# Block-sparse attention and a channel mixer in one kernel: PSUM as four slots of two banks for everything

## The chip, the cores and the metric

The kernel runs on one core of a Trainium2 chip, as one launch. The metric is the device time of that launch in microseconds (us). The engines are named as in the profile: PE (TensorE, the matmuls), ACT (ScalarE), DVE (VectorE), POOL (GpSimd) and SP (SyncE, which issues most DMAs). PSUM, where PE writes its results, has eight banks of 512 fp32 columns on 128 partitions.

## The reference

For 4 batches, 8 heads, 768 tokens and a head size of 64, attention with a block mask (blocks of 32 tokens), then a mixer over tokens and channels:

```python
scores = scale * np.matmul(q, k.transpose(0, 1, 3, 2))
mask = ...            # neighbours, first and last block, three sampled blocks per row of blocks
attn = softmax(np.where(mask, scores, -1e9))
x = np.matmul(attn, v) # heads side by side: batch, 768 tokens, 512 channels

h = x.transpose(0, 2, 1) @ U @ V          # rank 32, over the tokens
u = x + h.transpose(0, 2, 1)
out = u + np.maximum(u @ w_ch1, 0.0) @ w_ch2   # 512 -> 2048 -> 512 channels
```

## The kernel before, in words

Two heads are a pair; there are 16 pairs, four to a batch. Tokens are taken as six tiles of 128. All matmuls are in fp16 and add up in fp32.

- **Q K^T.** A pair is nine steps (`score`, L397): steps 0 to 5 take one key tile against queries 0 to 511, steps 6 to 8 take two key tiles against queries 512 to 767. Both heads of a step use 64 rows of the array each and write one PSUM tile of two banks. ACT takes exp of the whole step (L412, 128 x 1024) into an `e` buffer. In batch 0 the mask is added on PE (L404); later DVE multiplies `e` by the mask (L440, L445).
- **E V.** `values` (L478) multiplies a step's `e` with v, eight matmuls of 65 columns, the last column being the sum of the softmax. The pair's result lies in two accumulator tiles, one for token tiles 0 to 2 and one for 3 to 5. `divide` (L505, L508) divides on DVE into `x32`, and a copy to fp16 (`x16`, L524) follows. For the last pair of batch 0 DVE writes `x16` first and then `x32`, both from PSUM.
- **Token mix.** `amix` (L542) makes `a16` from x16 and U for a group of pairs (the first three pairs of a batch, then the fourth). `umix` transposes one block of 128 channels of x16 (L558) and adds V times a16 (L562), in two halves of 384 tokens; each half has its own PSUM tile and is copied to `uT` (L568) by ACT or DVE.
- **Channel products.** `up` (L592) multiplies w_ch1 with uT: for each two of the 16 rows of 128 channels three parts of 512 columns, each with a PSUM bank of its own and a Relu by DVE (L604) or ACT (L606) into `tT`. `down` (L615, L618) takes one token tile at a time through w_ch2, and DVE adds x32 (L625). The very last token tile goes in two halves (`down_half`, L637, L639).

PSUM is two tiles of two banks for the scores and four single banks for all else. The order is written out by a planner in the source: it keeps an estimated clock for each engine and for the banks (`take`, `give`, `drop`), and at each point issues the piece with the best rank that could start by then: a Q K^T visit, an E V visit, a mix piece or a channel piece. The instructions then run on each engine in that order; semaphores hold an instruction until what it needs is there. Once channel products are under way a Q K^T visit is two steps, held back by a due time so that the visits spread over the products. An E V visit is then six steps, or three. Batch b's products run among batch b+1's attention; the last batch's run alone at the end.

Of the kernel before, what the change touches and what calls it, by code (L numbers as in the profile page):

```python
# [22 lines left out]
def kernel(  # L23
# [32 lines left out]
    EB = 14  # L56
# [33 lines left out]
    tpool = ctx.enter_context(tc.tile_pool(name="tpool", bufs=9))  # L90
# [4 lines left out]
    ps_s = ctx.enter_context(tc.tile_pool(name="ps_s", bufs=2, space=PS))  # L95
    ps_f = ctx.enter_context(tc.tile_pool(name="ps_f", bufs=4, space=PS))

    def bank(shape, dtype):
        return ps_f.tile(shape, dtype, tag="ff", name="ff")
# [100 lines left out]
    def build_allow():  # L200

        pm = bank([P, NT, NB], FP32)
        for t in range(NT):
            nc.tensor.matmul(
                pm[:, t], biasf[:, t : S : NT], id16[:, 0:NB], start=True, stop=True
            )
        nc.vector.tensor_scalar(out=allow_k, in0=pm, scalar1=-1.0, scalar2=None, op0=ALU.is_ge)
# [31 lines left out]
    def keep_busy(n, cols):  # L239

        if not idle:
            idle.append(bank([P, 512], FP32))
        for _ in range(n):
            nc.tensor.matmul(
                idle[0][:, 0:cols], warm[:, 0:P], warm[:, 0:cols], start=True, stop=True
            )
# [37 lines left out]
    def transpose_part(name, t0, t1, evict):  # L284

        st = staged[name, 0]
        if t0 == 0:
            first[name] = new_qkT(name, 0)
        pt = bank([P, t1 - t0, P], FP16)
        for t in range(t0, t1):  # L290
            nc.tensor.transpose(  # L291
                out=pt[:, t - t0, :], in_=st[:, t].rearrange("p h d -> p (h d)"), identity=id16
            )
        evict(out=first[name][:, t0:t1], in_=pt)
# [41 lines left out]
    banks = [0.0, 0.0, 0.0, HELD]  # L336

    def take(n=1):
        banks.sort()
        return banks[n - 1]  # L340

    def give(t):

        banks.sort()
        banks[0] = t

    def drop(t):

        banks.sort()
        assert banks[-1] == HELD  # L350
        banks[-1] = t
# [7 lines left out]
    t_e, t_qk, t_x = {}, {}, {}  # L359
    sc_free = [0.0, 0.0]  # L360
# [28 lines left out]
    def score(si):  # L389
        n, s = divmod(si, SPP)  # L390
        qT, kT = qkT["q", n], qkT["k", n]
        sc_free.sort()
        ps = ps_s.tile([P, 2, 512], FP32, tag="sc", name="sc")
        biased = 2 <= si < SPB
        for g, q0, nq, at in parts(n, s):
            for h in range(2):
                nc.tensor.matmul(  # L397
                    ps[:, h, at : at + nq],
                    kT[h * D : (h + 1) * D, g * P : (g + 1) * P],
                    qT[h * D : (h + 1) * D, q0 : q0 + nq],  # L400
                    start=True, stop=not biased,
                )
            for h in range(2 if biased else 0):
                nc.tensor.matmul(  # L404
                    ps[:, h, at : at + nq],
                    biasf[h * D : (h + 1) * D, g : S : NT],
                    qhot[h * D : (h + 1) * D, q0 : q0 + nq],
                    start=False, stop=True,
                )
        t = on_pe(1024 if biased else 512, "rows", t_qk[n], sc_free[0], t_bias[0] if biased else 0.0)  # L410
        e = epool.tile([P, 2, 512], FP16, tag="e", name="e")
        nc.scalar.activation(out=e, in_=ps, func=AF.Exp, scale=0.125)  # L412
        sc_free[0] = t = on("ACT", 1024, t)
        if biased:
            t_e[si] = t
        else:
            masks.append((t, si, e))
            t_e[si] = max(t, clk["DVE"]) + FIX["DVE"] + COL["DVE"] * 1024 * 0.55 + HOP
        etiles[si] = e
# [32 lines left out]
    def values(sis):  # L452
# [9 lines left out]
        if n not in accs:  # L462
            if idle:
                idle.clear()
                drop(0.0)
            need = max(need, take(2))
            give(HELD)
            give(HELD)
            accs[n] = [0, [bank([P, NT // 2, 2, D + 1], FP32) for _ in range(2)], [0, 0]]
# [19 lines left out]
        if acc[0] == SPP:  # L489
            divide(n, 1, acc[1][1], t)  # L490
            del accs[n]

    def divide(n, hf, acc, t):
# [22 lines left out]
        if n == NPR - 1:  # L516

            t_x[n] = times(x16)
            drop(times(x32))
        else:  # L520
            t = times(x32)
            drop(t)
            eng = pick(nt * P, t, engines=("POOL", "DVE" if n < NPR else "ACT"))
            COPY[eng](out=x16[:, ts, c], in_=x32[:, ts, c])  # L524
            t_x[n] = on(eng, nt * P, t)

# [3 lines left out]
    def mixing(b, p0, p1):  # L530
# [8 lines left out]
        def amix():  # L539
            pa = bank([P, np_ * P], FP32)  # L540
# [10 lines left out]
        def umix(c, hf):  # L551

            if hf == 0:
                uT[c] = utp.tile([P, S], FP16, tag="uT", name="uT")
            pu = bank([P, HS], FP32)
            cs = slice(c * P, (c + 1) * P)
            for i in range(NT // 2):
                nc.tensor.matmul(  # L558
                    pu[:, i * P : (i + 1) * P], x16[:, hf * (NT // 2) + i, cs], id16,
                    start=(i == 0), stop=False,  # L560
                )
            nc.tensor.matmul(  # L562
                pu, a16[:, cs], Vt.rearrange("r t p -> r (t p)")[:, hf * HS : (hf + 1) * HS],
                start=False, stop=True,
            )
            tt = on_pe(HS * 2.3, "full", tm["a16"], take())
            eng = pick(HS, tt)
            COPY[eng](out=uT[c][:, hf * HS : (hf + 1) * HS], in_=pu)  # L568
            tm["uT"] = on(eng, HS, tt)
# [4 lines left out]
            (lambda: max(take(), tm["a16"]), lambda c=c, hf=hf: umix(c, hf))  # L574
            for c in range(p0, p1) for hf in range(2)
# [4 lines left out]
    def channels(b, uT, x32, a16, tm):  # L580
# [3 lines left out]
        def up(j, part):  # L584

            if part == 0:
                tT.append(tpool.tile([P, 2, S], FP16, tag="tT", name="tT"))
            pt = bank([P, 512], FP32)
            todo = [(part, 0, QA, 0)] if part < 2 else [(0, QA, QB, 0), (1, QA, QB, QB)]
            for i, q0, nq, at in todo:  # L590
                for c in range(NC):
                    nc.tensor.matmul(  # L592
                        pt[:, at : at + nq],
                        w1t[:, c, (2 * j + i) * P : (2 * j + i + 1) * P], uT[c][:, q0 : q0 + nq],
                        start=(c == 0), stop=(c == NC - 1),
                    )
            tt = on_pe(NC * 512, "full", tm["uT"], take())
            if part < 2:
                dst, src_ = tT[j][:, part, 0:QA], pt
            else:  # L600
                dst, src_ = tT[j][:, :, QA:S], pt.rearrange("k (i q) -> k i q", i=2)
            eng = pick(512, tt)
            if eng == "DVE":
                nc.vector.tensor_scalar_max(out=dst, in0=src_, scalar1=0.0)  # L604
            else:
                nc.scalar.activation(out=dst, in_=src_, func=AF.Relu)  # L606
            t_t[0] = on(eng, 512, tt)
            give(t_t[0])

        def down(t, j4):  # L610
            if j4 == 0:
                hold["at"] = take()
                give(HELD)
                hold[t] = bank([P, HD], FP32)
                nc.tensor.matmul(hold[t], Vt[:, t, :], a16, start=True, stop=False)  # L615
                on_pe(HD, "full", hold["at"])
            for j in range(JD * j4, JD * j4 + JD):
                nc.tensor.matmul(  # L618
                    hold[t], tT[j // 2][:, j % 2, t * P : (t + 1) * P], w2t[:, j, :],
# [3 lines left out]
            if j4 == NJ // JD - 1:  # L623
                of = opool.tile([P, HD], FP32, tag="of", name="of")
                nc.vector.tensor_add(out=of, in0=x32[:, t], in1=hold.pop(t))  # L625
                nc.sync.dma_start(
                    out=out[b].rearrange("(p t) c -> p t c", t=NT)[:, t, :], in_=of
                )
                drop(on("DVE", HD, tt))

        def down_half(t, hf):
# [4 lines left out]
            ph = bank([P, HD // 2], FP32)  # L636
            nc.tensor.matmul(ph, Vt[:, t, :], a16[:, c], start=True, stop=False)  # L637
            for j in range(NJ):
                nc.tensor.matmul(  # L639
                    ph, tT[j // 2][:, j % 2, t * P : (t + 1) * P], w2t[:, j, c],  # L640
# [10 lines left out]

        pieces = [
            (lambda: max(tm["uT"], take()), lambda j=j, part=part: up(j, part))
            for j in range(NJ // 2) for part in range(3)
        ]
        pieces += [
            ((lambda: max(t_t[0], take())) if j4 == 0 else (lambda: 0.0),
             lambda t=t, j4=j4: down(t, j4))
            for t in range(NT) for j4 in range(NJ // JD)
        ]  # L660
        if b == B - 1:
            pieces[-(NJ // JD) :] = [
                (lambda: max(t_t[0], take()), lambda hf=hf: down_half(NT - 1, hf))
# [38 lines left out]
    UP, DOWN = NC * 512, JD * HD  # L702
    NUP, NDOWN = 3 * NJ // 2, NT * NJ // JD
    FFN = NUP * UP + NDOWN * DOWN
    SPARE = 28000

    def left():

        d = min(len(chan), NDOWN)
        return d * DOWN + (len(chan) - d) * UP  # L710

# [3 lines left out]
    while step < NSTEP or ai < NSTEP or mixes or chan or waiting or groups:  # L715
# [13 lines left out]
        if step < NSTEP:  # L729
            n = step // SPP  # L730
            if n in t_qk and step - freed_steps() < EB:
                free = min(sc_free)
                if chan:

                    due = (step - SPB * (chan_done + 1)) / SPB * (FFN - SPARE)
                    free = max(*sc_free, now + due - (FFN - left()))

# [5 lines left out]
        if ai < NSTEP:  # L743
            n, at = divmod(ai, SPP)
            r = n % NPR
            end = n * SPP + (NW if at < NW else SPP)
# [6 lines left out]
            if todo and (ai + len(todo) == end or full or not chan):  # L753
                if not chan:
# [8 lines left out]
                if ok:  # L763
                    cands.append((rank, max(when, 0.0 if n in accs else take(2)), "av"))
# [6 lines left out]
        if what == "qk":  # L771
# [16 lines left out]
            for _ in range(2 if chan else 1):  # L788
# [51 lines left out]
```

## Time and profile before

| | |
|---|---|
| time, median of 3 runs | 299.05 us (298.02 to 299.06) |
| the profiled execution | 298.72 us, its span 296.8 us |
| granted PE clock | 0.999 |
| Q K^T matmuls, L397 | 384, busy 48.2 us; mask bias L404 92, 14.4 us |
| E V matmuls, L478 | 1152, busy 44.7 us |
| channel products, L592 and L618 | 512 and 368, busy 88.7 and 88.6 us |
| exp, L412 | 144, busy 138.7 us, 1025 ns each |
| Relu, L604 on DVE and L606 on ACT | 48 each, 690 and 597 ns each |

Matmuls are pipelined: the profile's duration of one (380 ns for 512 columns) is longer than the distance from one start to the next (216 ns), so busy shares of PE overstate, and the starts in the timeline tell what a stretch costs. In a group's row the last number is the engine's idle time just before those instructions, followed by what ended most of it; in the timeline a bracket gives the same for one entry. "Waits" lists give engine, tile and line that waited, what for, the sum in us, the number of waits and the longest.

### The profile page before, as it was taken

The numbers are of one execution on the slowest core, as the hardware profiler recorded it, in microseconds if no ns is written. First come the engines' busy times: TensorE is split into PE (matmuls) and PEld (weight loads), VectorE is DVE, ScalarE is ACT, GpSimd is POOL, SyncE is SP. The second block draws the span as 40 slices with busy tenths as digits, with TensorE's granted clock in tenths as the row PEclk, the third lists the DMA queues.
The fourth block names the chain that finished last, engine by engine and source line by source line (L and its number), as shares of the span: only waits on it lengthen the run. The fifth ranks groups of instructions, "written<-read, shape, count | busy, mean of one in ns | idle before, by whom it ended". The sixth has DMA issues, their size and how long they took to land.

```text
span 296.8 us, 6527 instructions
## 1 busy us (share of the span) xinstructions
PE 288.6 (97%) x2774; PEld 158.3 (53%) x2774; DVE 171.6 (58%) x308; ACT 183.2 (62%) x233; POOL 59.8 (20%) x75
## 2 busy tenths in 40 slices
PE   7998998999999999999999999999999999999995
PEld 2454654565635555565635555565645555665444
DVE  5662246787885666678775766678855664000112
ACT  4898977767655755767665664777666562664000
POOL 3734745230270403012040304003010000000000
PEclk9999999999999999999999999999999999999999
DMA  6689999999977428070356528061201101000111
GB/s 184 205 191 217 235 236 196 275 151 142 201 222 150 135 71 253 0 210 6 62 189 101 184 65 256 1 153 61 55 35 38 38 36 73 0 0 2 71 71 71
DMA packets 46596, 35.90 MB, mean 121 GB/s; under 512 B 26400, under 2 KB 43600, under 8 KB 46568
## 3 DMA queue, kind: packets, MB, share of 16 engines
q1 hardware_dynamic: 41056, 30.94, 41.4%
q0 software_dynamic: 5152, 4.39, 9.9%
q8 instruction: 21, 0.34, 0.5%
q10 hardware_dynamic: 360, 0.17, 0.2%
q14 instruction: 7, 0.06, 0.1%
HBM read 27.59 MB, written 6.29 MB: 114 GB/s over the span
## 4 chain that ended last, share of the span: by engine, by line
PE 90%; DMA 4%; ACT 3%; issue 1%; POOL 0%; DVE 0%; ACTq 0%; POOLq 0%
PE ff L592 29%; PE ff L618 27%; PE sc L397 12%; PE ff L478 11%; ACT e L412 3%; DMA raw_k<-in_k_dram 2%; PE ff L558 2%; PE ff L615 2%; PE ff L542 2%; PE ff L562 2%; PE sc L404 1%; DMA kT<-st_k 1%; PE ff L639 1%; DMA raw_q<-in_q_dram 1%; PE ff L291 0%
## 5 line engine op out<-in xcount | busy, mean ns | idle before, releaser
L412 ACT ACTIVATE e<-sc 128x1024 f16<-128x1024 f32 x144 | 138.7, 1025 | 23.8 <-PE sc L397 19.5
L592 PE MATMUL ff<-uT,w1t 128*128 128x256 f16 (+1 forms) x512 | 88.7, 326 | 0.4 <-ACT uT L568 0.4
L618 PE MATMUL ff<-w2t,tT 128*128 128x512 f16 x368 | 88.6, 379 | 0.0
L592 PEld LDWEIGHTS <-w1t 128*128 128x128 f16 x512 | 47.9, 98 | 38.8 <-issue 8.6
L440 DVE TENSOR_TENSOR e<-e,mask 128x1024 f16<-128x1024 f16 x74 | 55.4, 777 | 3.0 <-ACT e L412 2.9
L618 PEld LDWEIGHTS <-tT 128*128 128x128 f16 x368 | 34.1, 98 | 41.2 <-issue 5.5
L397 PE MATMUL sc<-qT,kT 64*128 64x512 f16 (+1 forms) x384 | 48.2, 327 | 1.9 <-DMA kT<-st_k 1.5
L478 PEld LDWEIGHTS <-e 128*128 128x128 f16 x1152 | 39.6, 97 | 16.1 <-issue 9.5
L478 PE MATMUL ff<-v,e 128*128 128x65 f16 x1152 | 44.7, 193 | 0.3 <-ACT e L412 0.3
L625 DVE TENSOR_TENSOR of<-x,ff 128x512 f32<-128x512 f32 x23 | 15.8, 687 | 48.6 <-PE ff L618 48.6
L604 DVE TENSOR_SCALAR tT<-ff 128x512 f16<-128x512 f32 x48 | 32.8, 690 | 15.7 <-PE ff L592 15.2
L606 ACT ACTIVATE tT<-ff 128x512 f16<-128x512 f32 x48 | 28.7, 597 | 21.4 <-PE ff L592 21.1
L146 POOL CAST st_q<-raw_q 128x768 f16<-128x768 f32 x15 | 13.8, 921 | 104.1 <-DMA raw_q<-in_q_dram 79.4
L524 ACT CAST x<-x 128x384 f16<-128x384 f32 x21 | 10.7, 512 | 35.0 <-DVE x L508 35.0
L397 PEld LDWEIGHTS <-kT 64*128 64x128 f16 x384 | 14.7, 94 | 20.5 <-issue 13.9
L445 DVE TENSOR_TENSOR e<-e,mask 128x1024 f16<-128x1024 f16 x36 | 24.3, 688 | 1.7 <-ACT e L412 1.7
L505 DVE RECIPROCAL rcp<-ff 128x6 f32<-128x6 f32 x32 | 6.2, 195 | 29.3 <-PE ff L478 28.9
L508 DVE TENSOR_TENSOR x<-ff,rcp 128x384 f32<-128x384 f32 (+1 forms) x34 | 18.8, 557 | 1.2
L137 POOL CAST v<-raw_v 128x768 f16<-128x768 f32 x16 | 15.0, 937 | 11.6 <-DMA raw_v<-in_v_dram 9.3
L146 POOL CAST st_k<-raw_k 128x768 f16<-128x768 f32 x15 | 13.3, 888 | 8.2 <-DMA raw_k<-in_k_dram 7.9
L404 PE MATMUL sc<-qhot,bias 64*128 64x256 f16 (+1 forms) x92 | 14.4, 320 | 0.0
L568 DVE CAST uT<-ff 128x384 f16<-128x384 f32 x18 | 9.7, 554 | 5.6 <-PE ff L562 5.4
(60 smaller groups left out, 121.6 us busy)
## 6 DMA issues: line engine op xcount, KB each, us to landing
raw_v<-in_v_dram SPq DMA_DIRECT2D x16, 384.0 KB, 5.9
out_dram<-of SPq DMA_DIRECT2D x23, 256.0 KB, 2.0
raw_q<-in_q_dram SPq DMA_DIRECT2D x15, 384.0 KB, 3.7
raw_k<-in_k_dram SPq DMA_DIRECT2D x15, 384.0 KB, 4.6
w1t<-in_moe_w_ch_dram POOLq DMA_DIRECT2D x4, 512.0 KB, 10.6
w2t<-in_moe_w_ch_dram POOLq DMA_DIRECT2D x4, 512.0 KB, 15.4
raw_q<-in_q_dram SPq DMA_DIRECT2D x1, 256.0 KB, 3.4
raw_k<-in_k_dram SPq DMA_DIRECT2D x1, 256.0 KB, 4.9
```

Source lines behind the costliest of these rows:

```text
L146: nc.gpsimd.tensor_copy(out=st, in_=raw[name, n].rearrange("p h (t d) -> p t h d", d=D))
L397: nc.tensor.matmul(ps[:, h, at : at + nq], kT[h * D : (h + 1) * D, g * P : (g + 1) * P], qT[h * D : (h + 1) * D, q0 : q0 + nq], start=True ...
L404: nc.tensor.matmul(ps[:, h, at : at + nq], biasf[h * D : (h + 1) * D, g : S : NT], qhot[h * D : (h + 1) * D, q0 : q0 + nq], start=False, s ...
L412: nc.scalar.activation(out=e, in_=ps, func=AF.Exp, scale=0.125)
L440: nc.vector.tensor_mul(out=e, in0=e, in1=m)
L445: nc.vector.tensor_mul(out=ev, in0=ev, in1=m)
L478: nc.tensor.matmul(acc[1][hf][:, t % (NT // 2), h, :], e[:, h, at + t * P - q0 : at + t * P - q0 + P], vt[:, g, h, 0 : D + 1], start=(done ...
L508: nc.vector.tensor_tensor(out=x[:, ts, c].rearrange("q t (h d) -> q t h d", d=D), in0=acc[:, :, :, 0:D], in1=rcp[:, :, :, None].broadcast_ ...
L592: nc.tensor.matmul(pt[:, at : at + nq], w1t[:, c, (2 * j + i) * P : (2 * j + i + 1) * P], uT[c][:, q0 : q0 + nq], start=(c == 0), stop=(c ...
L604: nc.vector.tensor_scalar_max(out=dst, in0=src_, scalar1=0.0)
L606: nc.scalar.activation(out=dst, in_=src_, func=AF.Relu)
L618: nc.tensor.matmul(hold[t], tT[j // 2][:, j % 2, t * P : (t + 1) * P], w2t[:, j, :], start=False, stop=(j == NJ - 1),)
```

## The change

PSUM becomes one pool of four slots, each of two banks, for scores, accumulators, mixes and products alike. A Q K^T visit among products is three steps, and goes as soon as the planner's estimate has slots for them and for the next product; the due time is gone. E V among products takes all nine steps of a pair in one visit, into the two banks of one slot. `umix` puts 512 tokens in bank 0 and 256 in bank 1 of one slot, each copied out as soon as it is written. `up` takes four rows of channels at a time in three parts, each part in a slot of its own (two halves of eight matmuls, one Relu of 1024 columns for both), and `down` takes two token tiles to a slot, with one add and one output DMA for both. The `e` buffers go from 14 to 16. The core of the diff (names and planner only lines left out):

```diff
-    EB = 14
+    EB = 16
...
-    ps_s = ctx.enter_context(tc.tile_pool(name="ps_s", bufs=2, space=PS))
-    ps_f = ctx.enter_context(tc.tile_pool(name="ps_f", bufs=4, space=PS))
-
-    def bank(shape, dtype):
-        return ps_f.tile(shape, dtype, tag="ff", name="ff")
+    ps = ctx.enter_context(tc.tile_pool(name="ps", bufs=4, space=PS))
+
+    def slot(dtype=FP32):
+
+        return ps.tile([P, 2, 512 if dtype == FP32 else 1024], dtype, tag="ps", name="ps")
...
-            accs[n] = [0, [bank([P, NT // 2, 2, D + 1], FP32) for _ in range(2)], [0, 0]]
+            both = slot()[:, :, 0 : NT * (D + 1)].rearrange("q i (t h d) -> q i t h d", h=2, d=D + 1)
+            accs[n] = [0, [both[:, i] for i in range(2)], [0, 0]]
...
-        def umix(c, hf):
-
-            if hf == 0:
-                uT[c] = utp.tile([P, S], FP16, tag="uT", name="uT")
-            pu = bank([P, HS], FP32)
+        def umix(c):
+
+            uT[c] = utp.tile([P, S], FP16, tag="uT", name="uT")
+            both = slot()
             cs = slice(c * P, (c + 1) * P)
-            for i in range(NT // 2):
+            ends = []
+            for q0, q1, eng in ((0, QA, "ACT"), (QA, S, "DVE")):
+                pu = both[:, q0 // QA, 0 : q1 - q0]
+                for t in range(q0 // P, q1 // P):
+                    nc.tensor.matmul(
+                        pu[:, t * P - q0 : (t + 1) * P - q0], x16[:, t, cs], id16,
+                        start=(t * P == q0), stop=False,
+                    )
                 nc.tensor.matmul(
-                    pu[:, i * P : (i + 1) * P], x16[:, hf * (NT // 2) + i, cs], id16,
-                    start=(i == 0), stop=False,
+                    pu, a16[:, cs], Vt.rearrange("r t p -> r (t p)")[:, q0:q1],
+                    start=False, stop=True,
                 )
...
+                if b > 0 or c < NPR - 1:
+                    eng = pick(q1 - q0, tt)
+                COPY[eng](out=uT[c][:, q0:q1], in_=pu)
...
-        def up(j, part):
+        def up(j, part, half):
...
+            if half == 0:
+                hold["at"] = take()
+                give(HELD)
+                hold["up"] = slot()
+            pt = hold["up"]
+            if part < 2:
+                todo = [(2 * part + half, 0, QA, 0)]
+            else:
+                todo = [(2 * half + i, QA, QB, i * QB) for i in range(2)]
...
-            eng = pick(512, tt)
+            eng = pick(1024, tt)
...
-        def down(t, j4):
+        def down(t, i, n, j4):
...
+                of = opool.tile([P, 2, HD], FP32, tag="of", name="of")
+                nc.vector.tensor_add(out=of[:, 0:n], in0=x32[:, ts], in1=po[:, 0:n])
                 nc.sync.dma_start(
-                    out=out[b].rearrange("(p t) c -> p t c", t=NT)[:, t, :], in_=of
+                    out=out[b].rearrange("(p t) c -> p t c", t=NT)[:, ts, :], in_=of[:, 0:n]
                 )
...
                 if chan:
 
-                    due = (step - SPB * (chan_done + 1)) / SPB * (FFN - SPARE)
-                    free = max(*sc_free, now + due - (FFN - left()))
+
+                    free = max(take(i + 1) - 512 * i for i in range(size + chan[0][2]))
...
-            end = n * SPP + (NW if at < NW else SPP)
+            end = (n + 1) * SPP
...
-            for _ in range(2 if chan else 1):
+            for i in range(size):
```

In the changed kernel the lines are: Q K^T L395 (bias L402), exp L410, masks L439 and L444, E V L477, `divide` L504 and L507, `amix` L541 (copy L546), `umix` L559 and L563 (copies L570), `up` L601 (Relu L616 and L618), `down` L630 and L633 (add L641), `down_half` L653.

## The prediction

> **What bounds the kernel now.** I read the page first: busy shares, then the chain that ended last.
>
> ```profile
> PE 288.6 (97%) x2774; PEld 158.3 (53%) x2774; DVE 171.6 (58%) x308; ACT 183.2 (62%) x233; POOL 59.8 (20%) x75
> PE 90%; DMA 4%; ACT 3%; issue 1%; POOL 0%; DVE 0%; ACTq 0%; POOLq 0%
> ```
>
> TensorE (PE) is the chain. No other engine is above 62%, so anything taken from or given to ACT and DVE alone is worth nothing; what counts is PE time and PE waiting. The waits of PE say how much waiting there is to win:
>
> ```profile
> PE sc L397 <- DMA kT<-st_k: 1.5, 1, 1.5
> PE ff L592 <- ACT uT L568: 0.4, 1, 0.4
> ```
>
> These are the first and third of that list; behind 49 us there is practically nothing. So a gain must come from PE work itself, and a new PE wait has nothing that hides it. Next, the PE timeline from 49 us on:
>
> ```profile
> 49.41 2.11 PE L592 MATMUL ff<-uT,w1t 128*128 128x512 f16 x13 [0.40 <-ACT uT L568]
> 51.46 0.61 PE L397 MATMUL sc<-qT,kT 64*128 64x512 f16 x4
> 52.00 2.77 PE L592 MATMUL ff<-uT,w1t 128*128 128x512 f16 x16
> 54.70 0.61 PE L397 MATMUL sc<-qT,kT 64*128 64x512 f16 x6
> ```
>
> A visit of Q K^T (L397, 64-row tiles) lasts 51.46 to 52.00, 0.54 us, for two steps whose matmuls stream in 2 x 0.216 = 0.43. The sixteen L592 behind it need 8 x 0.216 + 8 x 0.109 = 2.60 (starts of single matmuls) and take 2.70. By single starts, going into L397 costs 96 ns and coming out 92: 0.19 us a visit. That is the one PE cost this change reduces.
>
> **What it removes.** The instruction order of both kernels, cut at the first L592, shows 53 Q K^T visits behind it before and 36 after: 17 x 0.188 = **-3.2 us**. Two more unmasked steps (39 before, 41 after) stand ahead of that cut: 2 x 0.22 = **-0.44** behind it. All other matmuls, in columns and number, stay. E V in one visit saves nothing on PE: L478 to L592 shows no switching cost (L478's own 29 ns spacing goes on).
>
> **Off the path, taken at nothing.** Relu evictions halve in number and double in size (ACT 48 x 0.597 becomes 24 x 1.03; DVE 48 x 0.69 becomes 24 x about 1.22, an estimate from 0.690 for 512 and 1.04 ns a column). L592 hides them: a slot is filled in 1.73 us. If that cover went, each costs at most 0.5 more than now. The output adds and SP's output DMAs fall to about half; loads and transposes on SP keep their order. The last token still goes in two halves, so the tail behind PE (3.6 us) stays.
>
> **What it adds: a PE wait inside every channel mix.** Here the order with its semaphore waits decides. In `umix` both banks of one slot are filled, but the copy out of bank 0 is emitted before the transposes into bank 1. In the changed kernel's PE queue all 16 umix look like this:
>
> ```
> 2098 L563 Matmult ps_1727<-Vt_128,a16_1668 128x512
> 2100 L559 Matmult ps_1727<-id16_99,x16_1258 128x128 [waits DVE_49]
> ```
>
> The engine waited for is each time the one that copies bank 0 (ACT nine times, DVE seven), and the value awaited is the count which that copy itself reaches: dependence is kept by tile, and the slot is one tile. Before, the halves were two tiles:
>
> ```profile
> 44.47 0.33 PE L562 MATMUL ff<-Vt,a 128*128 128x384 f16 x1
> 44.63 0.33 PE L558 MATMUL ff<-id,x 128*128 128x128 f16 x3
> 44.83 1.22 DVE L568 CAST uT<-ff 128x384 f16<-128x384 f32 x2 [0.67 <-PE ff L562]
> 48.86 0.50 ACT L568 CAST uT<-ff 128x384 f16<-128x384 f32 x1
> 49.41 1.79 PE L592 MATMUL ff<-uT,w1t 128*128 128x512 f16 x10 [0.40 <-ACT uT L568]
> ```
>
> PE is at the next half (44.63) before DVE starts on the first (44.83), 0.36 us behind a 384-column start. And PE resumes 0.05 us behind a copy (48.86 + 0.50, 49.41). So the new wait is: 0.42 (0.36 plus 128 more columns) + the copy + 0.05, less the 0.216 that the matmul streams anyway. The copy of 512 columns:
>
> ```profile
> L604 DVE TENSOR_SCALAR tT<-ff 128x512 f16<-128x512 f32 x48 | 32.8, 690 | 15.7 <-PE ff L592 15.2
> L606 ACT ACTIVATE tT<-ff 128x512 f16<-128x512 f32 x48 | 28.7, 597 | 21.4 <-PE ff L592 21.1
> ```
>
> So 0.94 us for DVE and 0.84 for ACT, if that engine is free. PE executes in order: Q K^T, E V and the products queue behind it, and no work covers it.
>
> Batches 1 to 3, first three umix together (order: three steps, L633 x4, L541 x6, L633 x4, umix). With 0 at the three steps' start, ACT ends its third exp at 0.42 + 3 x 1.025 = 3.5 and is wanted at 4.1; DVE's masks end at 4.9 and it is wanted at 5.6. No queueing: ACT, DVE, ACT = 0.84 + 0.94 + 0.84 = 2.62, times 3 = 7.9.
> The fourth umix of each batch: batch 1, ACT is on the third exp until 3.5, wanted at 3.4, so 0.91, less 0.17 that L592 waited for uT before (spacing 385 instead of 216). Batch 2: the product queue is empty here (two one-step visits around L541 instead of products), so PE also waits about 0.1 for x16 and 0.48 for a16 behind an exp, then 0.94, less 0.17: 1.35. Batch 3: from L541's start to the first full-speed L592, 0.85 + 0.42 + 0.59 + 0.05 + 0.22 = 2.13 after against 1.52 before: 0.61. Together 2.7. Sum **+10.6**.
>
> **Batch 0, from its first L541 to L592.** Before this is 37.28 to 48.77 (L592's first three, then 0.56 waiting). The order after has L541 one step earlier, about 36.4. From there PE has, by rows, L541 1.4, nine Q K^T visits 5.4, eight E V steps 1.95, umix 2.64: 11.4 us of work. Its waits: three umix on DVE 2.8; the last one on ACT, behind an exp, 1.2; and a second wait of the same kind in E V, whose bank 1 steps wait until L507 has read bank 0 twice (reciprocal 0.20, 2 x 0.56, 0.2 to start): 1.5; x16 and a16 0.6. So 17.5, L592 at 53.9 against 48.77: **+5.1**. ACT, which sets the pace until 36 us (eleven exps in 10.19 us), has by then only one exp in reserve, so I take little of it as hidden; the same E V wait of pairs 0 to 2 (about 0.4 each) lies under the exps and costs nothing.
>
> **Do four slots suffice?** No row shows it. Walking the products behind the first L592 by rows, slots come free just in time: a third step starts at 5.61 and its slot is free at 5.43; E V wants one at 15.39, free at 15.2. Bounds: 0, and half an exp (0.5) at each of 36 visits, 18 us. The walk is nearest to 0, and a PE held up by umix only gives the slots more time: 0, with 3 us in the range.
>
> **The sum.** Profiled execution 298.72 (span 296.8 plus 1.9; the median is 299.05): 298.72 - 3.2 - 0.44 + 10.6 + 5.1 = **310.8 us**.
>
> **Rivals.**
> 1. *The bank-1 waits cost nothing* (faster). Then 298.7 - 3.2 - 0.4 = 295.1. For it: before, PE wrote one bank while DVE read another. The Trainium skill, page "PSUM — Partial Sum Buffer", section "PSUM bank collisions raise a hardware error", says guarding by bank and 32-partition quadrant is enough, and that different banks do not collide; a guard by its rule would give this rival's time, 295. The overlap at 44.8 agrees. Against it: the wait is in the built queue and names the copy. It decides if a wait is under 3.6 / 16 = 0.23 us; 0.42 of latency alone is more. Chance 0.07 (0.05 faster, 0.02 near zero).
> 2. *Slots run dry as well.* A third step half an exp late at every visit gives 310.8 + 18 = 329, at a third of them 317. It decides if copies come 0.2 later than my walk. The evenly spread exps speak for it, 36 visits without pacing against. Chance 0.10.
> 3. *Batch 0's waits hide under the exps.* ACT idles several times 0.5 us from 36 to 48 us, which speaks against. Then 310.8 - 5.1 = 305.7. Chance 0.06.
> 4. *PE's clock drops behind the pauses.* The first L244 matmuls stand 427 ns apart, later ones 216; eight such at 16 places would add 1.7 each, 338. Against it: granted clock 1.00 in every stretch, and full speed right behind a 1.66 us pause at 23.85. On the pages, "TensorE: Matmul & The Clock Gate", section "A second HAM failure mode: psum-queue depth-cycling", in the Trainium skill, speaks for this: short pauses between groups that cycle through banks were seen to throttle the clock. The 1.66 us pause here does not agree. Chance 0.02.
>
> The forecast has 0.75.
>
> **Range.** Low: batch 0's term halved (-2.6) and waits shorter by 0.2 each (-2.7): 305.5. High: slots 3 and 0.2 queueing on each of 12 umix, 2.4: 316.5. It leaves out rivals 1 and 4 and most of 2. A measurement of this kernel tells about 0.5% (1.5 us) from no change. Faster 0.05, same 0.02, slower 0.93.
>
> **What would show it.** In the profile after: PE waits with a new line L559 <- ACT and DVE L570, some 14 us in 16 pieces of 0.8 to 1.4; L477 <- DVE L507 about 1.5 at 45 us; first L601 near 54 us; L395 in 36 visits behind it, 0.19 saved each. Wrong if L559 waits under 4 us in sum, or if L395 or L601 wait for ACT L410 for several us.

## The result: 312.44 us, 4.5% slower

The changed kernel takes 312.44 us (median of six executions, 311.14 to 313.82), the kernel before 299.06 beside it (298.02 to 303.49): 1.045 times the time, interval 1.0405 to 1.050. The ratios here and below leave out executions more than 1.5% above the fastest of their kernel. The profiled execution took 313.55 us, its span 311.6. From the page of the kernel after, busy time and the chain that ended last:

```profile
PE 287.6 (92%) x2774; PEld 160.0 (51%) x2774; DVE 157.1 (50%) x261; ACT 192.4 (62%) x224; POOL 55.4 (18%) x72
...
PE 83%; ACT 4%; DVE 3%; DMA 1%; issue 1%; ACTq 0%
```

PE has the same 2774 matmuls and is even busy 1.0 us less than before, yet its share of the chain fell from 90% to 83%: the 15 us came mostly as waiting. The waits of PE in the kernel after (engine, tile, line, what for; sum in us, number, longest) say where:

```profile
PE ps L559 <- ACT uT L570: 6.5, 9, 1.1
PE ps L559 <- DVE uT L570: 5.5, 7, 0.8
PE ps L477 <- DVE x L507: 2.3, 4, 1.3
PE ps L395 <- DMA kT<-st_k: 1.9, 1, 1.9
...
PE ps L395 <- ACT e L410: 0.8, 2, 0.5
PE ps L559 <- ACT e L410: 0.4, 1, 0.4
```

The first two lines are new: 9 + 7 = 16 waits, one in each `umix`, each for the copy of bank 0 of the slot whose bank 1 is to be written. One of them, in the chain of the kernel after (start, duration):

```profile
104.90 0.23 PE ps L563
105.13 0.02 issue
105.16 0.59 ACT uT L570
105.75 0.04 issue
105.79 0.27 PE ps L559 x2
```

PE starts the matmul that ends bank 0 at its own rate (104.74 by the timeline; the chain shows it where the one before ends), the copy starts 0.42 us behind that start, lasts 0.59, and PE goes on 0.04 us behind it at 105.79. Without the wait the next transposes would have started 0.22 behind 104.74, at 104.96: 0.83 us lost. The list of waits counts less than that, because it takes a matmul as busy for its whole pipelined 0.38 us. By starts, that is by the distance from one matmul's start to the next, the 16 waits cost 14.6 us.

The last pair of batch 0, in the timeline of the kernel after (start, duration, and in the bracket the idle time before and its cause):

```profile
47.75 1.02 DVE L507 TENSOR_TENSOR x<-ps,rcp 128x384 f16<-128x384 f32 x2
48.82 0.40 PE L477 MATMUL ps<-v,e 128*128 128x65 f16 x8 [1.34 <-DVE x L507]
```

This is the second such wait: E V into bank 1 stands until both divisions have read bank 0, 1.5 us by starts.

Three steps to a visit, in the chain:

```profile
59.95 0.76 PE ps L601 x7
60.71 0.76 PE ps L395 x10
61.47 0.54 PE ps L601 x4
```

Ten Q K^T matmuls of 64 rows (one step of two, two of four) pass in 0.76 us. Two steps took 0.54 before, 0.81 for three. The 0.05 between is the entry into 64-row tiles, paid once for three steps instead of once for two; the way back, 0.09 a visit, lies in the product behind. And the doubled Relu, from the groups by form:

```profile
L618 ACT ACTIVATE tT<-ps 128x1024 f16<-128x1024 f32 x31 | 31.7, 1023 | 19.1 <-PE ps L601 19.1
...
L616 DVE TENSOR_SCALAR tT<-ps 128x1024 f16<-128x1024 f32 x17 | 20.8, 1224 | 26.9 <-PE ps L601 26.8
```

Both engines idle before them, waiting for PE, and PE's list has no wait for them: in this kernel they cost the end nothing.

By single starts the two profiled executions compare like this; the last columns are those of three experiments below.

| us | before | after | e1 | e3 | e7 |
|---|---|---|---|---|---|
| first `amix` matmul | 37.28 | 38.47 | 37.44 | 39.41 | 37.45 |
| from there to the first product at full speed | 11.49 | 17.74 | 14.47 | 13.96 | 12.88 |
| from there to PE's last matmul | 244.4 | 251.6 | 242.3 | 240.0 | 241.0 |
| median of all executions | 299.06 | 312.44 | 299.96 | 298.55 | 296.72 |

Before, three products at 48.21 stand ahead of a wait of 0.56 us; they are counted as if they stood behind it, so the second row ends at 48.77. After against before: 1.2 + 6.25 + 7.2 = 14.6 of the 14.8 us between the two profiled executions. The medians are 13.4 apart, and the 1.2 lies within the spread of starts told in the last section. The rows also don't hold quite the same work: 39 Q K^T steps stand ahead of the first product before, 41 in after and e1, 43 in e3, 42 in e7, and the first `amix` itself has 421 matmuls ahead of it before and in e7, 409 in after and e1, 429 in e3.

### The profile page after: what moved, and what is told of

The parts are those of the page before. It is cut to its first block, busy times and chain, and to the rows that moved or that the text cites. A ratio compares the mean times of both kernels' runs of the same rounds, so it can differ in the third digit from the quotient of the medians.

```text
span 311.6 us, 6447 instructions
## 1 busy us (share of the span) xinstructions
PE 287.6 (92%) x2774; PEld 160.0 (51%) x2774; DVE 157.1 (50%) x261; ACT 192.4 (62%) x224; POOL 55.4 (18%) x72
## 4 chain that ended last, share of the span: by engine, by line
PE 83%; ACT 4%; DVE 3%; DMA 1%; issue 1%; ACTq 0%
PE ps L601 27%; PE ps L633 26%; PE ps L477 10%; PE ps L395 10%; PE ps L559 3%; ACT e L410 2%; PE ps L563 2%; ACT uT L570 2%; PE ps L630 2%; DVE uT L570 2%; PE ps L541 1%; DMA kT<-st_k 1%; PE ps L655 1%; PE ps L402 1%; DVE x L507 1%
## 5 line engine op out<-in xcount | busy, mean ns | idle before, releaser
L410 ACT ACTIVATE e<-ps 128x1024 f16<-128x1024 f32 x144 | 137.5, 1030 | 30.5 <-PE ps L395 21.1
L633 PE MATMUL ps<-w2t,tT 128*128 128x512 f16 x368 | 87.7, 379 | 0.0
L601 PE MATMUL ps<-uT,w1t 128*128 128x256 f16 (+1 forms) x512 | 87.0, 326 | 0.0
L601 PEld LDWEIGHTS <-w1t 128*128 128x128 f16 x512 | 48.5, 98 | 35.6 <-issue 5.1
L439 DVE TENSOR_TENSOR e<-e,mask 128x1024 f16<-128x1024 f16 x74 | 56.5, 783 | 14.8 <-ACT e L410 14.7
L633 PEld LDWEIGHTS <-tT 128*128 128x128 f16 x368 | 34.3, 98 | 41.5 <-issue 5.1
L395 PE MATMUL ps<-qT,kT 64*128 64x512 f16 (+1 forms) x384 | 45.7, 327 | 3.1 <-DMA kT<-st_k 1.9
L477 PEld LDWEIGHTS <-e 128*128 128x128 f16 x1152 | 38.6, 97 | 13.7 <-issue 10.8
L477 PE MATMUL ps<-v,e 128*128 128x65 f16 x1152 | 42.2, 193 | 2.3 <-DVE x L507 2.3
L618 ACT ACTIVATE tT<-ps 128x1024 f16<-128x1024 f32 x31 | 31.7, 1023 | 19.1 <-PE ps L601 19.1
L616 DVE TENSOR_SCALAR tT<-ps 128x1024 f16<-128x1024 f32 x17 | 20.8, 1224 | 26.9 <-PE ps L601 26.8
L641 DVE TENSOR_TENSOR of<-x,ps 128x1024 f32<-128x1024 f32 (+1 forms) x12 | 14.1, 1175 | 39.9 <-PE ps L633 39.9
L395 PEld LDWEIGHTS <-kT 64*128 64x128 f16 x384 | 16.8, 94 | 24.4 <-issue 15.8
L444 DVE TENSOR_TENSOR e<-e,mask 128x1024 f16<-128x1024 f16 x36 | 24.2, 686 | 6.9 <-ACT e L410 6.9
L504 DVE RECIPROCAL rcp<-ps 128x6 f32<-128x6 f32 x32 | 6.1, 191 | 32.5 <-PE ps L477 32.4
L559 PE MATMUL ps<-id,x 128*128 128x128 f16 x96 | 10.3, 219 | 12.3 <-ACT uT L570 6.5
L507 DVE TENSOR_TENSOR x<-ps,rcp 128x384 f32<-128x384 f32 (+1 forms) x34 | 18.8, 557 | 1.2
L570 DVE CAST uT<-ps 128x256 f16<-128x256 f32 (+1 forms) x15 | 8.2, 549 | 18.2 <-PE ps L563 18.2
L559 PEld LDWEIGHTS <-x 128*128 128x128 f16 x96 | 7.6, 97 | 19.0 <-issue 17.8
```

Source lines behind the costliest of these rows:

```text
L395: nc.tensor.matmul(sc[:, h, at : at + nq], kT[h * D : (h + 1) * D, g * P : (g + 1) * P], qT[h * D : (h + 1) * D, q0 : q0 + nq], start=True ...
L410: nc.scalar.activation(out=e, in_=sc, func=AF.Exp, scale=0.125)
L439: nc.vector.tensor_mul(out=e, in0=e, in1=m)
L444: nc.vector.tensor_mul(out=ev, in0=ev, in1=m)
L477: nc.tensor.matmul(acc[1][hf][:, t % (NT // 2), h, :], e[:, h, at + t * P - q0 : at + t * P - q0 + P], vt[:, g, h, 0 : D + 1], start=(done ...
L507: nc.vector.tensor_tensor(out=x[:, ts, c].rearrange("q t (h d) -> q t h d", d=D), in0=acc[:, :, :, 0:D], in1=rcp[:, :, :, None].broadcast_ ...
```

## The experiments

Every one starts from the kernel after. They ran in several groups, each with runs of the kernel before beside it (medians 298.86 to 298.95), so ratios are to those.

**e1_copies_last: the waits alone.** `umix` fills both banks first, and copies both out after; nothing else is touched, and PE's instructions keep their order.

```diff
-                COPY[eng](out=uT[c][:, q0:q1], in_=pu)
+                out.append((eng, q0, q1, pu))
+            for eng, q0, q1, pu in out:
+                COPY[eng](out=uT[c][:, q0:q1], in_=pu)
```

> The changed kernel with one edit: umix issues the matmuls of both banks first and the two copies behind them; everything else stands in the same order. Theory (the loss is PE waiting inside umix for the copy out of bank 0): the 16 waits L559 <- L570, 14.6 us together, go; the copy of 512 starts 0.2 later, so that the first product of batches 0 and 3 may wait about 0.2 to 0.4 for uT. About 298.3 us (297 to 300). Rival (four shared slots and visits without pacing are what costs; a wait taken away comes back as a wait for a slot): 306 to 312, with L395 or L601 waiting for L410 instead.

Measured: 299.96 us (299.11 to 300.75), ratio 1.0037, interval 1.0004 to 1.0071. From the timeline of e1:

```profile
100.42 0.38 PE L563 MATMUL ps<-Vt,a 128*128 128x512 f16 x1
...
100.75 0.27 PE L563 MATMUL ps<-Vt,a 128*128 128x256 f16 x1
...
101.06 0.86 ACT L573 CAST uT<-ps 128x512 f16<-128x512 f32 x2 [1.04 <-PE ps L563]
```

PE ends both banks in one go (100.42 to 100.75), and the copy starts only behind them. The profiled execution is 13.5 us shorter than that of after, 1.0 of it ahead of the first `amix`. Behind that, with the same matmuls in the same order, it is 12.6: the 14.6 us of waits are gone, and 2.0 came back by starts, 1.3 of it as waits of the products for uT (0.6 in batch 0, 0.5 and 0.2 later), the rest in front of E V and Q K^T. So the 16 waits are the slowdown. But what is left is not faster than before: behind the first product it is 2.1 us shorter, and batch 0 loses 3.0 ahead of it. By single starts about half of these 3.0 is work that before does elsewhere (three more Q K^T steps and eight more E V matmuls in the stretch), and half is waiting, above all the 1.5 of E V.

**e8_two_slots: is it the tile or PSUM itself?** The two parts of `umix` get a slot each; the copies stay where they were.

```diff
-            both = slot()
...
-                pu = both[:, q0 // QA, 0 : q1 - q0]
+                pu = slot()[:, 0, 0 : q1 - q0]
```

> The changed kernel with one edit: the two parts of umix in a slot each (bank 0 of it), the copies issued where they were, right behind each part; PE's order is the same. Theory (PE waits because the slot is one tile, not because the copy needs PE to stand still): the 16 waits for the copy just issued go. In the runs of three umix six slots are wanted of four, so there PE waits for older copies instead, an estimated 0.5 to 1 us in each of batches 1 to 3. About 302 (300 to 303.5). Rival (PE can't write PSUM beside such a copy, or the copies are late anyway): 309 to 313.

Measured: 300.05 us (298.70 to 301.49), ratio 1.0040, interval 1.0015 to 1.0065. From its timeline:

```profile
99.81 0.38 PE L562 MATMUL ps<-Vt,a 128*128 128x512 f16 x1
...
100.22 0.59 ACT L569 CAST uT<-ps 128x512 f16<-128x512 f32 x1 [0.82 <-PE ps L562]
100.24 0.39 PE L558 MATMUL ps<-id,x 128*128 128x128 f16 x4
```

The next `umix` writes (from 100.24) while ACT reads the last one (100.22 to 100.81), and PE doesn't slow down: four transposes and their step to the next matmul take 0.23 us there (100.24 to 100.47), as they do ahead of the read (99.58 to 99.81). The wait belongs to the dependence by tile: two banks in one tile are one thing to wait for. The Trainium skill, page "PSUM — Partial Sum Buffer", section "PSUM bank collisions raise a hardware error", asks for a guard by bank and quadrant only; this run agrees that different banks need none. The price of using up slots twice as fast was smaller than expected: against e1, whose order is the same, PE waits by starts 0.31 us more in each of batches 1 to 3 (0.5 to 1 was expected) and 1.2 more in batch 0, and 1.3 less for uT.

**e5_small_bank_first: the size of the copy.** The bank with 256 tokens first, so that PE waits for the shorter copy.

```diff
-            for q0, q1, eng in ((0, QA, "ACT"), (QA, S, "DVE")):
+            for q0, q1, eng in ((QA, S, "DVE"), (0, QA, "ACT")):
```

> The changed kernel, umix with its two banks in the other order: the 256 tokens first, so that the second bank's transposes wait for a copy of 256 columns (ACT 0.37, DVE 0.42) and not of 512 (0.59, 0.69). Theory: each of the 16 waits is 0.31 + copy + 0.05 - 0.11, 0.62 to 0.68 instead of 0.84 to 0.95, together 4 us less: 308.5 (307 to 310). Rival (the waits aren't what costs): 311 to 313, the same time with shorter waits.

Measured: 307.24 us (306.61 to 307.74), ratio 1.030, interval 1.0252 to 1.0347. Its PE waits begin:

```profile
PE ps L559 <- DVE uT L570: 5.3, 10, 0.6
PE ps L559 <- ACT uT L570: 2.8, 6, 0.5
```

Still 16 waits, now 0.62 to 0.68 each by starts but for one of 0.81, 10.7 in sum. A wait shrinks with its copy (256 columns: ACT 372 ns, DVE 424; 512: 585 and 691). By the ratios the kernel won 4.5 us, of which the waits explain 14.6 - 10.7 = 3.9. The edit moved the planner's order as well: behind the first product there are 34 visits instead of 36, about 0.4 us by e4 below.

**e2_divide_last: the E V wait alone.** The division of half 0 moves to the end of the pair.

```diff
-        if before < NW <= acc[0]:
-            divide(n, 0, acc[1][0], t)
...
+            divide(n, 0, acc[1][0], t)
```

> The changed kernel with one edit: both halves of a pair are divided when the whole pair is added up, so that no E V matmul writes a slot from which DVE still has to read. umix stays as it is. Theory: the four waits L477 <- L507 (2.3 us by the PE waits, of which three of 0.3 stand where the prediction took the exps to hide them) go, the first L541 comes 1 to 1.5 earlier; x16 of the last pair of batch 0 comes later. The planner's order shifts a little (39 steps ahead of the first product, 34 visits behind). About 310 (308.5 to 312). If those waits were hidden under the exps: only the 1.3 us of the fourth, partly given back to x16, 311.5 to 312.5.

Measured: 311.52 us (median of three, 310.12 to 312.64; a fourth took 317.03), ratio 1.0441, interval 1.0375 to 1.0507. That can't be told from after (1.0452): the gain did not come, or was smaller than this comparison can show.

**e3_both: both together.** The edits of e1 and e2.

> The changed kernel with both edits (copies behind both banks, both divides at the end of a pair); the order is that of the kernel with the divides alone. Theory: what is left of the change is fewer Q K^T visits (34 against 53 behind the first product, 0.19 each, 3.6 us): 295 to 298, faster than the kernel before by about 1%. Rival (slots run dry): 304 to 310.

Measured: 298.55 us (297.20 to 302.23), ratio 1.0002, interval 0.9964 to 1.0039: above the 295 to 298 that were expected, and no faster than before. Its waits of PE show where the E V wait went:

```profile
PE ps L540 <- DVE x L506: 1.2, 2, 0.8
PE ps L477 <- ACT e L410: 1.0, 3, 0.6
```

L477 waits for the division in e1 four times, 2.4 us in sum, and here not at all. But `amix` (L540 here) now waits for the later division, 1.2 against 0.3, and E V for exps, 1.0 against 0.2. So 1.7 of 2.4 came back. A wait in front of work that needs the delayed result anyway is only moved.

**e6_divide_issued_late: the early E V waits.** As e1, with the divisions of pairs 0 and 1 (and one part of pair 3's) handed out at the end of the pair, while the planner is told the old times, so that PE's order is exactly that of e1.

```diff
-        nc.vector.reciprocal(out=rcp, in_=acc[:, :, :, D])
+        hold_or_issue(n < 2, lambda: nc.vector.reciprocal(out=rcp, in_=acc[:, :, :, D]))
...
+            hold_or_issue(n < 2 or n == 3 and x is x32, lambda: nc.vector.tensor_tensor(
```

> The changed kernel with the copies behind both banks, and in batch 0 the division of the first half of pairs 0 and 1 issued at the end of the pair, that of pair 3 without its x32 part until then; PE's order is the same to the instruction. Theory (the wait of E V for L507 isn't hidden under the exps): two waits of about 0.5 go ahead of the first L541, which then stands about 1 us earlier, and the wait of pair 3 shrinks by 0.55: about 298.4 (297.5 to 299.2), against 300.0 with the copies alone. Rival (hidden, as the prediction had it): only the 0.55, 299.2 to 300.

Measured: 300.06 us (298.40 to 301.05), ratio 1.0034, interval 1.0010 to 1.0058: nothing gained on e1. Its waits of PE begin:

```profile
PE ps L395 <- DMA kT<-st_k: 1.9, 2, 1.4
PE ps L477 <- DVE x L515: 1.2, 2, 0.9
```

Half of the E V waits are gone, and the first `amix` starts 0.24 earlier than in e1 (37.20 against 37.44): PE gets sooner to a Q K^T step whose keys have not landed, and waits for that DMA (1.9 against 1.3). The 0.5 that pair 3's wait lost came back as a longer wait in `amix` (0.54). My theory for this run, that these early waits set batch 0 back, fell. The prediction had them as hidden, and for the two that were moved that stands; pair 2's wait was left as it was.

**e4_both_two_steps: the visits.** As e3, with two steps to a visit among products, as before; the slots that must be free stay as for three.

```diff
-                size = 3 if chan else 1
+                size = 2 if chan else 1
...
-                    free = max(take(i + 1) - 512 * i for i in range(size + chan[0][2]))
+                    free = max(take(i + 1) - 512 * i for i in range(3 + chan[0][2]))
```

> The kernel with both edits (copies behind both banks, both divides at the end of a pair), and Q K^T among products back at two steps a visit (it still waits for the slots that three would need). 53 visits behind the first product, as in the kernel before, against 34. Theory (a visit costs 0.19 us of switching, on the path): 19 x 0.19 = 3.6 us above the run with both edits, about 302 (301 to 303.5). Rival (what the switching takes is waited for elsewhere anyway): 298 to 299.5.

Measured: 302.98 us (301.38 to 305.82), ratio 1.0144, interval 1.0102 to 1.0186; 53 visits behind the first product instead of 34. From the first product to the last matmul it takes 244.4 us against 240.0 in e3. Of the 4.4 us one Q K^T step more behind the first product is 0.2 and longer waits are 0.3, so 3.9 / 19 = 0.20 us a visit. The kernel before takes 244.4 there too, with 53 visits. It has three steps more in that stretch than e4 (0.65 us) and as much less waiting. So behind the first product the visits are most of the gain of the change; the rest of it, steps done ahead of the first product, is paid there.

**e7_slots_from_products: batch 0.** As e1, but until the first product PSUM is as before (two tiles of two banks for scores, four single banks for the rest); the four slots open there.

```diff
-    ps = ctx.enter_context(tc.tile_pool(name="ps", bufs=4, space=PS))
+    first_pools = ctx.enter_context(ExitStack())
+    ps_s = first_pools.enter_context(tc.tile_pool(name="ps_s", bufs=2, space=PS))
+    ps_f = first_pools.enter_context(tc.tile_pool(name="ps_f", bufs=4, space=PS))
+    slots2 = []
...
-        sc = slot()
+        sc = slot() if slots2 else ps_s.tile([P, 2, 512], FP32, tag="sc", name="sc")
```

> The changed kernel with the copies behind both banks, and batch 0 with PSUM and order as before (two score tiles, four banks, halves of umix and of the accumulators in tiles of their own); the four slots begin with the first channel product. 34 visits behind it. Theory (the change gains behind the first product and loses ahead of it): the first product at 48.8 plus one visit of three steps, 0.85, then 240 us to the last matmul as in the run with both edits, then 5.5: about 295.1 (294 to 297), faster than the kernel before by 1%. Rival (the stretch ahead isn't lost to PSUM's split, or handing over the banks costs as much): 298 to 300.

Measured: 296.72 us (295.60 to 297.05), ratio 0.9919, interval 0.9896 to 0.9942: 0.8% under the kernel before, a small gain but clear of the interval. From its page and from its waits of PE:

```profile
PE 284.3 (96%) x2774; PEld 160.2 (54%) x2774; DVE 152.2 (52%) x260; ACT 193.4 (66%) x225; POOL 57.5 (19%) x72
```

```profile
PE ps L403 <- ACT uT L611: 1.0, 1, 1.0
```

The wait is the handover: the first slot opens only when the last of the early banks has been copied out. Batch 0's stretch is 12.88 us, 1.0 of it this wait and 0.75 a visit of three steps, against 14.47 in e1; behind it the kernel keeps the short 241.0.

## Why the prediction was right

The forecast was 310.8 us with 305.5 to 316.5; 312.44 lies in it, and the likeliest case is the one that came. By its own terms the range was 0.3 narrower at both ends (twelve waits of 0.2 are 2.4, so 305.8 and 316.2), which changes nothing.

- **The `umix` waits, the step that decides.** Right in number (16), cause and size: 0.84 for ACT and 0.94 for DVE were worked out, 0.836 and 0.945 measured, ACT, DVE, ACT in each group of three as forecast. Batches 1 to 3 were to lose 10.6; their twelve waits measure 10.5, and batch 0's four 4.1. That they are the cause was argued; e1 shows it (12.6 us less behind the first `amix` with PE's order kept), e8 that the tile decides and not the bank.
- **One fourth `umix` was read wrongly.** Batch 2's was to wait for x16 and a16 besides; it waited 0.4 for a slot held by an exp. Batch 3's came as worked out: from `amix` to the first product it takes 2.14 (262.96 to 265.10) where 2.13 was forecast, against 1.52 before.
- **Visits.** Taken at 0.188 each and so 3.2 in sum; e4 gives 0.20, which for 17 visits is 3.5.
- **Batch 0.** First `amix` to first product: 17.5 worked out, 17.74 measured, and the waits in it one by one: the three on DVE 2.8, the last on ACT 1.3 for 1.2, the last pair's E V wait 1.5 as forecast. Two of the three earlier E V waits lay under other work (e6). But the start of that stretch was put at 36.4 and came at 38.47. This is the term that was mis-sized, +2.1: the order was read as if `amix` one step earlier also came earlier in time. PE is not what sets that time. With the same order of PE's instructions up to there, `amix` started at 35.85 in e5, 37.20 in e6, 37.44 in e1 and 38.47 in after. In after PE waited 1.9 us for a key DMA and, earlier, 1.0 for a cast of keys on POOL; e5's list has neither.
- **Slots.** Taken as never dry, with 3 us in the range. They ran dry at one visit (83.6 us, 1.2 by starts) and at batch 2's `umix` (0.4): rival 2 was no more than that.
- **The sum behind the first product.** 7.0 worked out (10.6 - 3.2 - 0.4), 7.2 measured. By the measured terms it is 10.5 for the twelve waits, 0.3 for batch 3's a16 and 1.6 for slots, less 0.9 that the kernel before waits in its own mixes (uT 0.17 in each of three batches, a16 0.35), 3.5 for visits and 0.4 for steps: 7.6, or 0.4 more than measured. That 7.0 came so near is in part luck: the slots' 1.6 was left out, and smaller errors of the other sign make up for most of it.
- **Rivals.** Rival 1's condition, a wait under 0.23, was off by four times; its time of 295 is 1.6 us under what e7 reaches with the waits gone and batch 0 left alone. Rival 3's 305.7 failed with the four waits of 4.1 us in batch 0. Rival 4 did not come behind any of the 16 pauses of the profiled execution of after: the granted clock is 1.00, and the products of 512 columns behind them start 216 ns apart. What the Trainium skill says in the page "TensorE: Matmul & The Clock Gate", section "A second HAM failure mode: psum-queue depth-cycling", cited for that rival, is of short pauses between groups of matmuls; sixteen pauses of about a microsecond, some with only one `umix` between them, do not agree with it in this execution. Three other executions of after have a mean clock of 0.987 to 0.994, and no trace shows where it fell; the last section has a trace of e2 in which it fell among such pauses.

One change held two prices of opposite sign: fewer visits, about -3.5 us, and a mix in two banks of one tile, about +15.

## What to carry to other kernels

When several banks are put into one tile, emit all writes into it ahead of its first read, or give each bank its own tile: a read in the middle makes PE wait for the write's latency, the whole copy and the restart, whatever the banks are. Read such waits from the built order with its semaphores, price them from one row of the same copy, and multiply by the places where nothing else can run on PE. Weigh a new PSUM layout stage by stage: with the waits gone it is worth 2.1 us among the products in e1 and 4.4 in e3, the stretch ahead of the first product grows by 3.0 and 2.5, and only changing over between the two (e7) came out faster than before.

## What the runs showed of the hardware

The windows of PE in e3 (stretch, its length, busy time, number, granted clock, DMA share, GB/s):

```profile
core 0: us, PE busy (x), PEclk, DMA share, GB/s
23.80:25.70 1.90, 0.25 (x9) 1.00 0.44 97
25.70:27.20 1.50, 1.50 (x19) 0.99 1.01 337
27.20:30.60 3.40, 3.40 (x32) 0.50 0.76 224
30.60:34.00 3.40, 3.40 (x56) 1.00 0.94 199
```

PE pauses about 1.85 us for a load, works 1.5 us at full speed, and then runs 3.4 us at half the clock: 32 matmuls where the next 3.4 us hold 56 (of mixed sizes). In e4 the same stood behind a pause of 2.9 us, at 41.9 to 45.3. Pauses of 1.66 us (before) and 2.1 us (after) in the same stage had nothing behind them, so the length alone doesn't tell. The Trainium skill, page "TensorE: Matmul & The Clock Gate", section "HAM oscillation — how this bites in real kernels", gives "no PE-idle gaps >~3.4µs" as the rule; shorter gaps were followed by the drop here, and the measurement decides. In the one profiled execution of e2 (317.03 us, mean clock 0.973) half the clock was granted from 40.2 to 50.4 us, behind a pause of 2.6 us and through the `umix` pauses at 43 and 47 us, and again from 57.2 to 64.0; its twelve `umix` pauses behind that left the clock at full speed. One such stretch lowers an execution's mean clock to 0.994, and the kernel before shows that mean in some of its executions as well. What triggers it stays open. The column of the granted clock doesn't show all of it: the first L244 matmuls stand 427 ns apart under a granted 1.00, so read the starts as well.

The start of batch 0 varies by 2.6 us (35.85 to 38.47) between kernels whose PE order is the same up to there (after, e1, e5, e6, e8), and the waits of PE that differ are those for keys and queries: their casts, and the DMA that brings kT. In such a load-bound stage a single profile's start is not good to better than that.
